# Attention, experts and gated MLP on one core: a pair's six value products as one team, and the second pair's keys and queries loaded ahead of w_in

## The chip, the core and the metric

The kernel runs on one core of a Trainium2 chip. The core has five engines that run side by side, each with its own queue of instructions: TensorE (PE, matmuls; PEld is its weight load), VectorE (DVE), ScalarE (ACT), GpSimd (POOL) and SyncE (SP, which here only issues transfers). They meet by semaphores. The metric is the device time of one launch in microseconds; before it is 493.17 us, the median of three runs (492.27 to 494.79).

## What is computed

```python
# attention: 4 batches, 12 heads, 448 positions, head width 64
scores = scale * np.matmul(q, k.transpose(0, 1, 3, 2))
scores = cap * np.tanh(scores / cap)
scores = scores - np.max(scores, axis=-1, keepdims=True)
attn = np.exp(scores)
attn = attn / (np.sum(attn, axis=-1, keepdims=True) + 1e-09)
return np.matmul(attn, v).astype(np.float32)
...
# 4 experts, each a causal attention of width 64 over x (768 wide); a token's best 2 are mixed
a = np.exp(scores)
a /= a.sum(-1, keepdims=True) + 1e-09
ye = a @ v @ wo[e]
...
# gated MLP: h = gelu(x @ w_in); u, v = halves of h; v normed, mixed over positions by w_sg
gated = u * v_s
return (x + gated @ w_out).astype(np.float32)
```

The attention's output is the experts' x, and theirs is the MLP's. w_in comes as 64-bit numbers, and the kernel multiplies it ahead of time with the experts' output weights.

## The kernel before

The attention goes through 24 pairs of heads (4 batches, 6 pairs each); two heads of width 64 share the 128 partitions. Positions are 448 = 3 x 128 + 64. For pair n the scores come in four blocks named s_n_0 to s_n_3: three of 128 keys each for both heads, and a fourth with the 64 keys left over, which serves two neighbouring pairs at once. Names in the program are s, batch, pair, block, number; the profile leaves batch and buffer number out and writes s. Each block is two banks of PSUM, and there are two such tiles (`ps_s`, bufs=2). `scores` (line 588) computes a block on TensorE, then ScalarE takes its tanh into p (tile p_n_0 holds blocks 0 and 1, p_n_1 blocks 2 and 3) and the exponential over the whole of p. VectorE adds up the blocks into pb, from which TensorE takes the row sums (`sums`, 650).

`values` (621) multiplies the exponentials with the values. For an even pair that is six products into po: three blocks of 128 keys (KB = 3) times two heads, which lie side by side in TensorE as tiles of 128 rows by 64 columns. For an odd pair there are first four products of the leftover keys of both pairs (operand vt, tiles of 64 by 64), and then six. A score block uses tiles of 64 by 128. In float32 each product is two passes, so a product of one block for both heads is four instructions in the profile (x4), and two in the order (x2).

`slot` (675) does one pair: it loads, computes the scores of pair i and the values of pair i - 1, and between them runs side work, which in the first ten slots is `prepare_weights` (1086): w_in in twelve parts u = 0 to 11, each loaded (wi_0w and so on), turned from 64 bits into a float32 (`convert`: tiles wi0m and wi0e, on VectorE, the first step of u > 1 on ScalarE) and multiplied with wt on TensorE (w2ps). Later slots have the projections (qk), the transposes (tr) and the expert attention (a, av) of the batch that is finished as side work.

All this is first recorded and not issued. `Agenda` (77) keeps for each operation its engine, an estimate of how long it takes and what it needs; `run` (398) lists the recorded operations by the order of a planner, `order`, which goes forward in time and picks for each engine what can begin first, by four sets of rules of which the one that ends first is kept. Each engine then has a fixed order of instructions. On TensorE the planner forms teams: products that follow one another, have the same tile shape and lie in cells of the array that don't overlap (line 265). `begin` (275) lets a team's first product start only when the operands of all its members are there. Before, the two products of a key block are one team, and the next block's, which use the same cells, another.

The hardware knows nothing of teams. Each engine takes its queue strictly in the order written, and an instruction waits at its head for its own semaphores only.

Loads go through SP's queue, with eight transfers in flight. The first pair is loaded by `load_pair` (536), which ends in

```python
            load_w(0)
...
        return qp, kp, load_v(b, hp)
```

so the order of the first transfers is keys of pair 0, first part of w_in, values of pair 0 (vv, vt), keys, queries and values of pair 1.

Of the kernel before, what the change touches and what calls it, by code (L numbers as in the profile page):

```python
# [41 lines left out]
def drain(gen):  # L42
    for _ in gen:
        pass
# [32 lines left out]
class Agenda:  # L77


    LATENCY = {"pe": 230.0, "act": 60.0, "dve": 60.0, "pool": 100.0, "sp": 60.0}  # L80
    SLACK, MARGIN = 1000.0, (150.0, 200.0)
    STATE = ("slots", "queue", "where", "left", "free", "grid", "fresh", "cfg", "bank", "lock", "pipe", "kept")
    RULES = ((100.0, 0.0, 100.0), (100.0, 0.0, None), (100.0, 20.0, 100.0), (60.0, 0.0, 100.0))
    OVERLAP = {"act": 100.0, "dve": 80.0, "pool": 27.0, "sp": 0.0}
# [15 lines left out]
    def state(self, new):  # L100
        held = {k: [list(x) for x in v] if k in ("grid", "fresh") else
                {q: list(x) if isinstance(x, list) else x for q, x in v.items()} if isinstance(v, dict) else v
                for k, v in ((k, getattr(self, k)) for k in self.STATE)}
        return held, {i: (list(self.ops[i]["took"]), *[self.ops[i].get(k) for k in ("at", "end")]) for i in new}
# [27 lines left out]
    def add(self, eng, f, args, kw):  # L132
        i, name = len(self.ops), f.__name__
# [7 lines left out]
        after, tiles = set(), []  # L141
# [15 lines left out]
        for these, those in self.behind.items():  # L157
            if any(x.startswith(these) for x in tiles):
                after.update(self.of[those])
        op = dict(i=i, eng=eng, call=lambda: f(*args, **kw), after=after, tiles=set(tiles), took=[], port=False,  # L160
                  rank=i + self.late)
        n = max(x.free_size() for x in ins[:2] + outs[:1])
        psum = any(x.space == PSUM for x in ins + outs)
# [8 lines left out]
        elif eng == "pe":  # L172
# [5 lines left out]
            r, c = half(st.partition_size()), half(outs[0].partition_size())  # L178
            if name == "transpose":
                r = c = 4  # L180
# [23 lines left out]
    def order(self, new, by_level, floor):  # L204
        ops, uses = self.ops, self.uses
# [4 lines left out]
        for i in reversed(new):  # L210
            op = ops[i]
            took = op["dur"] + self.LATENCY[op["eng"]]
            if "bytes" in op:
                took = 2100.0 + op["extra"] + op["pipe"]
            elif op["eng"] == "pe":
                took = op["dur"] + (0.0 if any(ops[j]["eng"] == "pe" for j in then[i]) else 220.0)
# [42 lines left out]
        gang, team = {}, []  # L259
        for i in new:  # L260
            op = ops[i]
            if op["eng"] != "pe":
                continue
            r, c, r0, c0 = op["cell"]
            if (r, c) == (4, 4) or not team or (r, c) != ops[team[0]]["cell"][:2] or any(
                    abs(r0 - ops[j]["cell"][2]) < r and abs(c0 - ops[j]["cell"][3]) < c for j in team):
                team = []
            team.append(i)
            gang[i] = team
# [46 lines left out]
        while todo:  # L316
            best = None
            for e, pool in pools.items():
# [13 lines left out]
                if e == "pe":  # L332
                    t, i = max(near, key=lambda x: (ops[x[1]]["bank"] == self.bank, ops[x[1]]["key"], -x[1]))
                elif e == "sp":
                    t, i = min(near, key=lambda x: x[1])
                else:
                    t, i = max(near, key=lambda x: (ops[x[1]]["key"], -x[1]))
# [3 lines left out]
            t, i = best  # L341
            op = ops[i]
# [11 lines left out]
            if e == "pe":  # L354
                r, c, r0, c0 = op["cell"]
# [64 lines left out]
def build(ctx: ExitStack, tc: tile.TileContext, a: dict):  # L420
# [35 lines left out]
    agenda = Agenda(tc)  # L456
# [4 lines left out]
    def dma(*args, **kw):  # L461
        return sp.dma_start(*args, **kw) if agenda.on else nc.sync.dma_start(*args, **kw)
# [24 lines left out]
    def scale(with_keys):  # L487
        dve.memset(tsc, 0.0)
        act.activation(tsc, tsc, AF.Tanh)
        dve.reciprocal(tsc, with_keys)  # L490
        dve.tensor_copy(capt, with_keys)
        dve.tensor_scalar(tsc, tsc, 1.0 / math.sqrt(D), None, op0=ALU.mult)
# [34 lines left out]
    def load_v(b, hp):  # L527

        vv = at.tile([128, 2, KB, D], F32, tag="vv", name=f"vv{b}_{hp}", bufs=3)
        dma(vv, a["v"][b, :, 2 * hp:2 * hp + 2])  # L530
        if hp % 2 == 0:
            vt[b, hp // 2] = at.tile([128, 2, D], F32, tag="vt", name=f"vt{b}_{hp}", bufs=2)
            dma(vt[b, hp // 2], a["vt"][b, hp // 2])
        return vv

    def load_pair(b, hp):

        qp = at.tile([128, S], F32, tag="qp", name=f"qp{b}_{hp}", bufs=3)
        kp = at.tile([128, S + 1], F32, tag="kp", name=f"kp{b}_{hp}", bufs=3)
        if (b, hp) == pairs[0]:  # L540
            for c in (slice(0, S // 2), slice(S // 2, S)):
                act.dma_start(qp[:, c], a["qT"][b, :, hp, c])
            for c in (slice(0, 128), slice(128, S + 1)):
                dma(kp[:, c], a["k_cap"][:, c])
            scale(kp[:, S:])
            load_w(0)
        else:
            dma(kp[:, :S], a["kT"][b, :, hp, :])
            dma(qp, a["qT"][b, :, hp, :])
        return qp, kp, load_v(b, hp)  # L550

    PARTED = 12

# [2 lines left out]
    def part(i):  # L556

        if PARTED <= i < len(pairs):
            parts[i] = []
            for x, t, h, l in zip(ld[i], "qk", 'va', 'vv'):  # L560
                xh, xl = (at.tile([128, S], F32R, tag=t + p, name=f"{t}{p}{i}", bufs=2) for p in "hl")
                rnd(h, xh, x[:, :S])
                rest(l, xl, x[:, :S], xh)
                parts[i].append((xh, xl))
# [56 lines left out]
    def values(b, hp, vv):  # L621


        i, w = hp // 2, hp % 2
        if w == 0:
            po = ps_o.tile([128, 512], F32, tag="po", name=f"po{b}_{hp}")
            for c in range(KB):
                for j in range(2):
                    mm(po[64 * j:64 * j + 64, :S], vv[:, j, c, :], pend[b, hp][c // 2][:, j, c % 2, :],
                       start=(c == 0), stop=False)  # L630
                yield 805.0
            po_t[b, i] = po
            return
        po = (po_t.pop((b, i)), ps_g.tile([128, 512], F32, tag="g", name=f"po{b}_{hp}"))
        v, p = vt.pop((b, i)), ptail.pop((b, i))
        for t in range(2):
            r = slice(64 * t, 64 * t + 64)
            for j in range(2):
                mm(po[t][64 * j:64 * j + 64, :S], v[r, j, :], p[r, j, :], start=(t == 1), stop=(t == 0))
        yield 805.0  # L640
        os_t[b, i] = ao.tile([128, 2, S], F32, tag="os", name=f"os{b}_{hp}", bufs=5)
        act.activation(os_t[b, i][:, 0, :], po[0][:, :S], AF.Copy)
        for c in range(KB):
            for j in range(2):
                mm(po[1][64 * j:64 * j + 64, :S], vv[:, j, c, :], pend[b, hp][c // 2][:, j, c % 2, :],
                   start=False, stop=(c == KB - 1))
            yield 805.0
        act.activation(os_t[b, i][:, 1, :], po[1][:, :S], AF.Copy)

    def sums(b, i):  # L650
        g = ps_g.tile([128, 512], F32, tag="g", name=f"sum{b}_{i}")
        for j in range(4):
            mm(g[32 * j:32 * j + 32, :S], ones, pend[b, 2 * i + j // 2][2][:, j % 2, :], start=True, stop=True)
        rs = sums_t[b, i] = ao.tile([128, S], F32, name=f"rs{b}_{i}", tag="rs", bufs=1)
        rnd("avv"[i], rs, g[:, :S])
        yield 870.0
# [15 lines left out]
    pairs = [(b, hp) for b in range(B) for hp in range(HP)]  # L672
    ld = {}

    def slot(i, side):

        if i == 0:
            ld[0] = load_pair(*pairs[0])  # L680
            ld[1] = load_pair(*pairs[1])
        if i + 2 < len(pairs):
            qk = [at.tile([128, n], F32, tag=t, name=f"{t}{i + 2}", bufs=3) for t, n in (("qp", S), ("kp", S + 1))]
            b, hp = pairs[i + 2]
            dma(qk[1][:, :S], a["kT"][b, :, hp, :])
            dma(qk[0], a["qT"][b, :, hp, :])
            ld[i + 2] = qk
        part(i + 1)
        if i < len(pairs):
            first = scores(*pairs[i], 0, *ld[i][:2])  # L690
            drain(islice(first, 2))
            side("a")
            drain(first)
        else:
            side("a")
        side("w")
        if i:
            b, hp = pairs[i - 1]
            drain(values(b, hp, ld.pop(i - 1)[2]))
        if 0 < i < len(pairs) - 1:  # L700
            b, hp = pairs[i + 1]
            ld[i + 1] = (*ld[i + 1], load_v(b, hp))
        side("a")
        if i < len(pairs):
            drain(scores(*pairs[i], 1, *ld[i][:2], None if i % 2 else ld[i + 1][:2]))
        if i == len(pairs):
            drain(sums(B - 1, HP // 2 - 1))
            spread(B - 1, HP // 2 - 1)
        side("p")
        if 0 < i < len(pairs):  # L710
            b, hp = pairs[i - 1]
            if hp % 2 == 1:
                drain(sums(b, hp // 2))
        if i < len(pairs):
            add_up(*pairs[i])
        side("n")
# [435 lines left out]
    with tc.tile_pool(name="pre", bufs=2) as pre:  # L1152
# [7 lines left out]
        load_w, beside_pre = prepare_weights(pre)  # L1160
# [282 lines left out]
```

## Time and profile before

| | |
|---|---|
| median of 3 runs | 493.17 us (492.27 to 494.79) |
| profiled execution | 492.94 us |
| its span | 491.1 us, 7664 instructions |
| TensorE busy | 484.3 us, 99% |
| VectorE busy | 362.2 us, 74% |
| ScalarE busy | 325.1 us, 66% |
| GpSimd busy | 47.8 us, 10% |

The profile is of one execution; its span is what the engines' records cover, and 1.8 us of the execution lie around it. A busy share is a mean over stages: the attention is over by about 250 us, and ScalarE's share falls from there on. Times in a row are from the span's start. Where one engine's next instruction starts before the end that a row gives for the last one, the two overlap in the engine, so the distance between starts is what an instruction takes of the engine's time.

### The profile page before, as it was taken

Reading aid. Unit: us, or ns where it says so; the run is one execution under the profiler, and the core shown is the slowest. Engines: PE = TensorE matmul, PEld = TensorE weight load, DVE = VectorE, ACT = ScalarE, POOL = GpSimd, SP = SyncE. Lnnn points to the kernel's source line nnn. Section 1 sums busy time; section 2 is a strip of 40 time slices with the busy share of each in tenths; the row PEclk is TensorE's granted clock in tenths of the full one; section 3 lists DMA queues with packets and bytes.
Section 4 is the critical chain, followed back from the end, with each engine's and each line's share of the span. In section 5 each row is a group of like instructions: output and inputs, shape, how many; then the busy total and the mean of one; then the engine's idle time right before and its main releaser. Section 6 shows DMA issues by size and latency. Waiting matters only on the chain.

```text
span 491.1 us, 7664 instructions
## 1 busy us (share of the span) xinstructions
PE 484.3 (99%) x2723; PEld 332.8 (68%) x2723; DVE 362.2 (74%) x796; ACT 325.1 (66%) x555; POOL 47.8 (10%) x61
## 2 busy tenths in 40 slices
PE   9999999999999999999999999999999999999996
PEld 3333333456556657675658797687898998999996
DVE  4999999777899898998756789729979929707000
ACT  6999968999869887788736766647555625513201
POOL 0000000000200303100201302033010200100000
PEclk9999999999999999999999999999999999999999
DMA  8986556555161624141046320161010110110122
GB/s 285 351 308 186 168 133 184 174 151 168 42 176 43 191 61 155 50 131 40 33 128 193 93 81 33 45 240 50 0 39 1 39 37 1 56 57 19 57 75 75
DMA packets 37301, 53.38 MB, mean 109 GB/s; under 512 B 7696, under 2 KB 32272, under 8 KB 37264
## 3 DMA queue, kind: packets, MB, share of 16 engines
q1 hardware_dynamic: 36832, 52.56, 33.9%
q8 instruction: 21, 0.34, 0.3%
q10 hardware_dynamic: 432, 0.34, 0.2%
q14 instruction: 16, 0.13, 0.1%
HBM read 41.97 MB, written 10.83 MB: 108 GB/s over the span
## 4 chain that ended last, share of the span: by engine, by line
PE 90%; DVE 4%; ACT 3%; DMA 1%; issue 1%; SPq 0%; ACTq 0%
PE o L449 18%; PE po L449 12%; PE qk L449 12%; PE s L449 11%; PE sp L449 7%; PE v L449 7%; PE a L449 4%; PE hv L449 4%; PE hu L449 4%; PE w2ps L449 4%; PE av L449 3%; PE tr L449 3%; ACT p L449 2%; PE sum L449 2%; DMA wi_0w<-in_w_in_dram 1%; DVE pb L449 1%
## 5 line engine op out<-in xcount | busy, mean ns | idle before, releaser
L449 ACT ACTIVATE p<-s,tsc 128x896 f32<-128x896 f32 (+1 forms) x85 | 82.3, 999 | 13.1 <-PE s L449 13.0
L449 ACT ACTIVATE p<-p,capt 128x1792 f32<-128x1792 f32 (+1 forms) x48 | 76.9, 1605 | 0.7
L449 PE MATMUL po<-p,vv 128*64 128x448 f32 x288 | 59.9, 548 | 0.1
L449 DVE TENSOR_TENSOR pb<-pb,p 128x896 f32<-128x896 f32 (+1 forms) x48 | 54.1, 1127 | 5.7 <-ACT p L449 5.1
L449 PE MATMUL s<-qp,kp 64*128 64x448 f32 (+2 forms) x244 | 46.4, 566 | 0.2
L449 PEld LDWEIGHTS po<-p,vv 128*64 128x64 f32 x288 | 18.3, 136 | 38.1 <-issue 30.1
L449 DVE CUSTOM_DVE_ANT_0 a<-a,neg 128x128 f32<-128x128 f32 (+3 forms) x56 | 24.7, 471 | 21.3 <-PE a L449 19.2
L449 ACT ACTIVATE ob<-o 128x448 f32<-128x448 f32 (+1 forms) x24 | 12.4, 534 | 37.9 <-PE o L449 34.9
L449 PE MATMUL qk<-xh,wqk_h 128*128 128x448 f32 x96 | 36.5, 380 | 0.1
L449 PEld LDWEIGHTS s<-qp,kp 64*128 64x128 f32 (+1 forms) x244 | 16.4, 171 | 28.0 <-issue 13.5
L449 PE MATMUL qk<-xh,wqk_l 128*128 128x448 f32 x96 | 34.9, 364 | 0.0
L449 ACT ACTIVATE pe<-a,m 128x128 f32<-128x128 f32 (+3 forms) x56 | 27.4, 496 | 9.7 <-DVE m L449 4.9
L449 DVE SCALAR_TENSOR_TENSOR vs<-sp,gln,bsg 128x448 f32<-128x448 f32 x16 | 10.7, 679 | 30.0 <-PE sp L449 29.9
L449 DVE TENSOR_TENSOR pb<-p 128x896 f32<-128x896 f32 x24 | 26.4, 1099 | 7.6 <-ACT p L449 4.8
L449 ACT ACTIVATE gsu<-gsu 128x448 f32<-128x448 f32 x16 | 9.3, 579 | 25.4 <-DVE gsu L449 25.4
L449 PE MATMUL a<-qk 64*128 64x128 f32 (+3 forms) x128 | 25.1, 452 | 0.9 <-ACT qk L449 0.6
L449 PEld LDWEIGHTS qk<-xh,wqk_h 128*128 128x128 f32 x96 | 18.0, 187 | 8.7 <-issue 3.7
L449 PE MATMUL sp<-sg_h,vh 128*128 128x448 f32 x64 | 23.6, 370 | 0.0
L449 PE MATMUL sp<-sg_l,vh 128*128 128x448 f32 x64 | 23.4, 365 | 0.0
L449 PE MATMUL qk<-xl,wqk_h 128*128 128x448 f32 x96 | 22.0, 364 | 0.0
L449 POOL TENSOR_TENSOR rstd<-rstd,mhalf 128x1 f32<-128x1 f32 (+1 forms) x16 | 11.4, 712 | 102.2 <-DVE rstd L449 102.0
L449 PE MATMUL v<-wvg_h,xh 128*128 128x260 f32 x72 | 21.1, 293 | 0.2 <-ACT pe L449 0.2
(272 smaller groups left out, 1200.7 us busy)
## 6 DMA issues: line engine op xcount, KB each, us to landing
rb<-rd SPq DMA_DIRECT2D x24, 224.0 KB, 4.2
kp<-in_kT_dram SPq DMA_DIRECT2D x23, 224.0 KB, 4.0
qp<-in_qT_dram SPq DMA_DIRECT2D x23, 224.0 KB, 4.2
out_dram<-ob SPq DMA_DIRECT2D x23, 224.0 KB, 1.9
vv<-in_v_dram SPq DMA_DIRECT2D x24, 192.0 KB, 3.5
wuw<-in_w_out_dram SPq DMA_DIRECT2D x5, 384.0 KB, 4.2
wud<-wuw SPq DMA_DIRECT2D x10, 192.0 KB, 3.6
ws<-in_wqk_dram SPq DMA_DIRECT2D x4, 384.0 KB, 5.5
```

The lines of the kernel that those rows point to most:

```text
L449: return tc.keep_in_program_order(f(*args, **kw))
```

## The change

Two things. Products recorded with the same value of `join` now form one team even where they use the same cells, so that the planner lets the first of a pair's six products start only when the operands of all six are there. And `load_pair` no longer loads values and w_in; `slot` loads, at its first call, keys and queries of both first pairs, then the first part of w_in, then the values of both.

```diff
+    join = None
...
-        op = dict(i=i, eng=eng, call=lambda: f(*args, **kw), after=after, tiles=set(tiles), took=[], port=False,
+        op = dict(i=i, join=self.join, eng=eng, call=lambda: f(*args, **kw), after=after, tiles=set(tiles), took=[], port=False,
                   rank=i + self.late)
...
-            if (r, c) == (4, 4) or not team or (r, c) != ops[team[0]]["cell"][:2] or any(
+            same = team and op["join"] is not None and op["join"] == ops[team[0]]["join"]
+            if not same and (r, c) == (4, 4) or not team or (r, c) != ops[team[0]]["cell"][:2] or not same and any(
                     abs(r0 - ops[j]["cell"][2]) < r and abs(c0 - ops[j]["cell"][3]) < c for j in team):
                 team = []
...
-            load_w(0)
...
-        return qp, kp, load_v(b, hp)
+        return qp, kp
...
+            agenda.join = f"po{b}_{hp}"
             for c in range(KB):
                 for j in range(2):
                     mm(po[64 * j:64 * j + 64, :S], vv[:, j, c, :], pend[b, hp][c // 2][:, j, c % 2, :],
                        start=(c == 0), stop=False)
                 yield 805.0
+            agenda.join = None
...
             ld[0] = load_pair(*pairs[0])
             ld[1] = load_pair(*pairs[1])
+            load_w(0)
+            ld[0] = (*ld[0], load_v(*pairs[0]))
+            ld[1] = (*ld[1], load_v(*pairs[1]))
```

The six products of an odd pair get the same two lines. The work is the same; the planner orders much of TensorE, ScalarE and VectorE anew up to about 250 us of the span, and from there TensorE's order is the same as before.

TensorE in the first 20 us, before: s0_1_0 is block 0 of pair 1 of batch 0, po0_0 the products of pair 0, p0_0_0 and p0_0_1 its exponentials.

```order
L449 MATMUL s0_0_3_131<-qp0_1_115,kp0_1_116 64x448 x2
L449 MATMUL po0_0_141<-p0_0_0_120,vv0_0_113 64x448 x4
L449 MATMUL s0_1_0_135<-qp0_1_115,kp0_1_116 128x448 x2
L449 MATMUL s0_1_1_136<-qp0_1_115,kp0_1_116 128x448 x2
L449 MATMUL po0_0_141<-p0_0_1_129,vv0_0_113 64x448 x2
L449 MATMUL po0_0_141<-p0_0_1_129,vt0_0_114 64x448 x2
L449 MATMUL po0_1_156<-p0_0_1_129,vt0_0_114 64x448 x2
L449 MATMUL s0_1_2_145<-qp0_1_115,kp0_1_116 128x448 x2
```

After:

```order
L451 MATMUL s0_0_3_131<-qp0_1_112,kp0_1_113 64x448 x2
L451 MATMUL s0_1_0_135<-qp0_1_112,kp0_1_113 128x448 x2
L451 MATMUL s0_1_1_136<-qp0_1_112,kp0_1_113 128x448 x2
L451 MATMUL po0_0_141<-p0_0_0_120,vv0_0_115 64x448 x4
L451 MATMUL po0_0_141<-p0_0_1_129,vv0_0_115 64x448 x2
L451 MATMUL po0_0_141<-p0_0_1_129,vt0_0_116 64x448 x2
L451 MATMUL po0_1_156<-p0_0_1_129,vt0_0_116 64x448 x2
L451 MATMUL s0_1_2_145<-qp0_1_112,kp0_1_113 128x448 x2
```

The first four products of pair 0 (eight instructions of the profile) stood ahead of s0_1_0 and s0_1_1, and now stand behind these, together with the other two.

VectorE's way to the second part of w_in, wi1m, before: wi0_1w is the part as loaded, pb0_0 the sums of pair 0's exponentials.

```order
L449 TENSOR_SCALAR wi1m_137<-wi0_1w_126 128x512
L449 TENSOR_SCALAR wi1m_137<-wi1m_137 128x512 x2
L449 SCALAR_TENSOR_TENSOR wi1m_137<-wi0_1w_126,wi1m_137 128x512
L449 TENSOR_SCALAR wi1e_138<-wi1m_137 128x512
L449 TENSOR_TENSOR pb0_0_125<-pb0_0_125,p0_0_1_129 128x896
L449 SCALAR_TENSOR_TENSOR wi1e_138<-wi0_1w_126,wi1e_138 128x512
L449 TENSOR_TENSOR pb0_0_125<-pb0_0_125,p0_0_1_129 64x896
L449 TENSOR_TENSOR wi1m_137<-wi1m_137,wi1e_138 128x512
L449 TENSOR_SCALAR wi2m_151<-wi2m_151 128x512
```

After:

```order
L451 TENSOR_SCALAR wi1m_137<-wi0_1w_126 128x512
L451 TENSOR_TENSOR wi0m_123<-wi0m_123,wi0e_124 128x512
L451 TENSOR_SCALAR wi1m_137<-wi1m_137 128x512 x2
L451 TENSOR_TENSOR pb0_0_125<-pb0_0_125,p0_0_1_129 128x896
L451 SCALAR_TENSOR_TENSOR wi1m_137<-wi0_1w_126,wi1m_137 128x512
L451 TENSOR_TENSOR pb0_0_125<-pb0_0_125,p0_0_1_129 64x896
L451 TENSOR_SCALAR wi1e_138<-wi1m_137 128x512
L451 TENSOR_SCALAR wi2m_151<-wi2m_151 128x512
L451 SCALAR_TENSOR_TENSOR wi1e_138<-wi0_1w_126,wi1e_138 128x512
L451 TENSOR_SCALAR wi2m_151<-wi2m_151 128x512
L451 TENSOR_TENSOR wi1m_137<-wi1m_137,wi1e_138 128x512
```

Two steps of the third part, wi2m, and the end of the first, wi0m, now stand between the steps of wi1m; its steps are also further apart.

TensorE in the third batch, around the projection qk0_1_1 of the expert work, before: s2_3_2 and s2_4_0 are score blocks, po2_2 products.

```order
L449 MATMUL po2_2_965<-p2_2_1_944,vv2_2_911 64x448 x2
L449 MATMUL s2_3_2_970<-qh15_932,kh15_934 128x448 x2
L449 MATMUL s2_3_2_970<-ql15_933,kh15_934 128x448 x2
L449 MATMUL s2_3_2_970<-qh15_932,kl15_935 128x448 x2
L449 MATMUL s2_4_0_984<-qh16_956,kh16_958 128x448 x2
L449 MATMUL s2_4_0_984<-ql16_957,kh16_958 128x448 x2
L449 MATMUL s2_4_0_984<-qh16_956,kl16_959 128x448 x2
L449 MATMUL qk0_1_1_971<-xh0_290,wqk_h_76 128x448
```

After, from the end of that projection (tr are transposes of the expert work):

```order
L451 MATMUL tr0_0_1_0_972<-ident_73,pe0_0_1_0_872 128x128
L451 MATMUL tr0_0_1_0_972<-ident_73,pe0_0_1_1_884 128x128 x2
L451 MATMUL tr0_0_1_2_973<-ident_73,pe0_0_1_2_907 128x128 x3
L451 MATMUL po2_2_965<-p2_2_0_936,vv2_2_911 64x448 x4
L451 MATMUL po2_2_965<-p2_2_1_944,vv2_2_911 64x448 x2
L451 MATMUL s2_3_2_970<-qh15_932,kh15_934 128x448 x2
L451 MATMUL s2_3_2_970<-ql15_933,kh15_934 128x448 x2
L451 MATMUL s2_3_2_970<-qh15_932,kl15_935 128x448 x2
L451 MATMUL s2_4_0_984<-qh16_956,kh16_958 128x448 x2
L451 MATMUL s2_4_0_984<-ql16_957,kh16_958 128x448 x2
L451 MATMUL s2_4_0_984<-qh16_956,kl16_959 128x448 x2
L451 MATMUL tr0_0_1_3_974<-ident_73,pe0_0_0_3_915 128x128 x4
```

Two score blocks stood ahead of the projection, with a third of pair 2's products; after, all three products of pair 2 and both blocks stand behind it and its transposes.

## Rows read from the trace of the kernel before

**Rows 1.** The page: busy time of the engines, and the chain that ended last

```profile
PE 484.3 (99%) x2723; PEld 332.8 (68%) x2723; DVE 362.2 (74%) x796; ACT 325.1 (66%) x555; POOL 47.8 (10%) x61
...
PE 90%; DVE 4%; ACT 3%; DMA 1%; issue 1%; SPq 0%; ACTq 0%
```

**Rows 2.** Busy time by stretch: start:end, length, busy us of each engine, PE clock, DMA

```profile
10.00:33.00 23.00, 22.77 (x115) 7.40 (x113) 22.73 (x39) 22.78 (x26) 0.00 (x0) 1.00 1.00 356
...
60.00:140.00 80.00, 80.00 (x460) 39.82 (x459) 67.36 (x120) 68.79 (x90) 3.79 (x4) 1.00 0.53 148
140.00:162.00 22.00, 21.80 (x150) 14.27 (x150) 20.55 (x39) 19.46 (x28) 2.62 (x3) 1.00 0.35 96
162.00:260.00 98.00, 97.15 (x661) 62.93 (x658) 80.42 (x192) 71.38 (x124) 12.51 (x12) 1.00 0.33 100
```

**Rows 3.** Timeline of SP: start us, us, queue line op out<-in xcount

```profile
7.22 0.33 SPq L449 DMA_DIRECT2D wi_1w<-in_w_in_dram  x1
...
8.13 0.43 SPq L449 DMA_DIRECT2D wt<-in_woT_dram  x1
...
9.15 0.37 SPq L449 DMA_DIRECT2D negf<-in_c_neg_dram  x1
```

**Rows 4.** Timeline of VectorE: start us, us, engine line op out<-in shapes xcount [idle before]

```profile
7.23 0.43 DVE L449 TENSOR_SCALAR wi0m<-wi_0w 128x512 int32<-128x512 int32 x1 [2.95 <-DMA wi_0w<-in_w_in_dram]
7.69 0.89 DVE L449 TENSOR_SCALAR wi0m<-wi0m 128x512 f32<-128x512 f32 x2
...
17.21 0.68 DVE L449 TENSOR_TENSOR wi1m<-wi1m,wi1e 128x512 f32<-128x512 f32 x1
17.82 0.41 DVE L449 TENSOR_SCALAR wi2m<-wi2m 128x512 f32<-128x512 f32 x1
```

**Rows 5.** Timeline of ScalarE at the start

```profile
8.17 1.79 ACT L449 ACTIVATE p<-p,capt 128x1792 f32<-128x1792 f32 x1
9.87 1.89 ACT L449 ACTIVATE p<-s,tsc 128x896 f32<-128x896 f32 x2
11.79 1.79 ACT L449 ACTIVATE p<-p,capt 128x1792 f32<-128x1792 f32 x1
```

**Rows 6.** Timeline of TensorE, 10 to 34 us

```profile
10.07 1.72 PE L449 MATMUL po<-p,vv 128*64 128x448 f32 x8
11.73 1.77 PE L449 MATMUL s<-qp,kp 64*128 64x448 f32 x8
13.63 0.97 PE L449 MATMUL po<-p,vv 128*64 128x448 f32 x4
14.54 0.98 PE L449 MATMUL po<-p,vt 64*64 64x448 f32 x8
15.45 1.77 PE L449 MATMUL s<-qp,kp 64*128 64x448 f32 x8
17.15 1.12 PE L449 MATMUL w2ps<-wi0m,wt 128*128 128x512 f32 x2
18.12 1.02 PE L449 MATMUL w2ps<-wi1m,wt 128*128 128x512 f32 x2
...
22.49 2.48 PE L449 MATMUL po<-p,vv 128*64 128x448 f32 x12
24.89 0.98 PE L449 MATMUL s<-qp,kp 64*64 64x448 f32 x8
...
31.87 2.14 PE L449 MATMUL s<-qp,kp 64*128 64x448 f32 x8
```

**Rows 7.** Timeline of ScalarE beside the projection of the third batch

```profile
149.52 1.89 ACT L449 ACTIVATE p<-s,tsc 128x896 f32<-128x896 f32 x2
151.30 1.04 ACT L449 ACTIVATE p<-p,capt 128x896 f32<-128x896 f32 x1
152.24 0.54 ACT L449 ACTIVATE qk<-qk 128x448 f32<-128x448 f32 x1
```

**Rows 8.** Timeline of TensorE behind that projection

```profile
152.82 0.66 PE L449 MATMUL tr<-ident,pe 128*128 128x128 f32 x4 [0.20 <-ACT qk L449]
```

More of the change, by code (lines that the diff above doesn't have):

```diff
@@ L642, in values @@
         act.activation(os_t[b, i][:, 0, :], po[0][:, :S], AF.Copy)
+        agenda.join = f"po{b}_{hp}"
         for c in range(KB):
@@ L647, in values @@
             yield 805.0
+        agenda.join = None
         act.activation(os_t[b, i][:, 1, :], po[1][:, :S], AF.Copy)
```

## The prediction

> **What bounds the kernel now.** I read the shares of the engines first. The reader is to see one number: TensorE is busy for 484.3 of 491.1 us, and the chain that ended last is TensorE for 90% [rows 1]. So the end moves by what the change puts into or takes out of TensorE's own row: rounds, changes of tile shape, and gaps. Second, the same by stage: from 10 to 33 us all three of TensorE, VectorE and ScalarE are within 0.3 us of full, and from 140 to 162 us VectorE and ScalarE have only 1.5 and 2.5 us of slack in 22; from 60 to 140 they have 11 to 13 us in 80 [rows 2]. An edit that makes VectorE or ScalarE late therefore shows at once in the first stretch and around 150 us, and is swallowed between. Nothing of TensorE's arithmetic is removed, so a gain can come only from gaps and tile shape changes, and before 260 us the gaps are few: TensorE's slack is 0.23 us in 10 to 33, none in 60 to 140, 0.2 in 140 to 162 and 0.85 in 162 to 260 [rows 2]. That limits the gain, before any detail is read, to these gaps and what the shape changes cost.
>
> **The load order.** SP has eight transfers in the air; each further issue starts when the transfer eight places earlier has landed. So SP's issue times tell landings: w_in's first part at 7.22, the head's last value tile before 8.13, second keys and second queries by 9.15 [rows 3]. VectorE confirms the first: it has been idle 2.95 us when it starts on w_in at 7.23 [rows 4]. Keys and queries took 9.15 - 8.13 = 1.02 us of the queue; now they go ahead, and w_in's first part lands about 1.0 us later, at 8.25. Bounds: 0 (if the transfers share the engines rather than follow one another) and 1.92 (9.15 itself). Everything behind vt_0 lands as before, since the same bytes are ahead of it. What the earlier keys buy: the second half of s_0_3 can be computed sooner, but ScalarE only reads it with the second of two tanh started at 9.87, and it runs through from 8.17 [rows 5]; so nothing.
>
> **The head of the products.** Before, TensorE uses the time in which it has no free score tile for the first eight product instructions (10.07), then does s_1_0 and s_1_1, then the other products when the second exponential ends at 11.79 + 1.79 = 13.58 [rows 5, 6]. As one team of a pair's products they can't go first any more: s_1_0 and s_1_1 come ahead, and these need the two score tiles. The first tanh of 9.87 ends at about 10.86, the second at 11.76 (the row holds two, 1.89). So s_1_0 starts at 10.91, s_1_1 at 11.81 and ends at 12.66 (1.70 for two blocks, 15.45 to 17.15). The twelve product instructions take 2.40 (22.49 to 24.89), to 15.06; the exponential of 13.58 is in time for the last four. The vt products take 0.91, to 15.97, where before had 15.45 [rows 6]: **+0.52**. That already has one tile shape change less in it: eight and four instructions apart took 1.66 + 0.91 = 2.57 against 2.40.
>
> **The first w_in products.** TensorE then does two score blocks (1.70) and the wi0m product (0.97) and wants wi1m at 18.64. VectorE before goes from 7.23 to 17.89 without a pause, 10.66 us, until wi1m is there [rows 4]. After, two wi2m steps stand ahead of it (0.41 long, some 0.35 apart, +0.7), while about five steps no longer directly follow the one that they read (0.46 from 7.23 to 7.69 for a step of 0.43, but 0.61 from 17.21 to 17.82 for one of 0.68: about 0.1 each, -0.5 to -0.6). So 10.75 or so from 8.25: 19.0, and TensorE starts at 19.1: **+0.5**. Bounds: 0 (w_in lands as before) and 1.3 (it lands at 9.15). Everything queued behind this product on TensorE, which takes its queue in order, waits with it.
>
> **The rest of the first two batches.** Joined products leave stretches in which score blocks follow one another with no products between. There are two score tiles, so a third block waits until ScalarE has emptied the first. Before shows one such case: at 31.87 two blocks take 2.14 where 1.77 is usual, +0.37 [rows 6]. In the new order I find three that look as tight (s_3_1 near 29 us; the second w_in part, where wi8m comes late, near 57; s_2_2 of the second batch near 79), and the old one is gone, since w_in products stand there now: 3 x 0.37 - 0.37 = **+0.74**. Lower bound 0 (each absorbed), upper 1.5 (twice as long each).
>
> **Around 150 us.** Before, both score blocks s_3_2 and s_4_0 of the third batch stand ahead of the projection qk, so ScalarE does their two tanh and an exponential (149.52 to 152.24) while TensorE projects [rows 7]; TensorE then waits only about 0.2 us, at 152.82 [rows 8]. After, the projection comes first, then the joined products, s_3_2, s_4_0. From the end of s_3_2 ScalarE has tanh, tanh, the half exponential, the copy of a transpose to pt and another tanh before s_4_3 can start: 0.89 + 0.89 + 0.94 + 0.54 (taken as the copy at 152.24) + 0.92 = 4.2, with some 0.2 for starting. TensorE has s_4_0, the transposes, s_4_1, a, s_4_2 and the vt products: three blocks of some 0.75 and 0.6, 0.15 and 0.9, 3.9 us. The last of these takes the PSUM tile that the pt copy frees, so it waits first; I take 1.0 us for both waits, less the 0.2 to 0.4 that go: **+0.7**. Bounds 0 and 1.75 (the two waits end to end).
>
> **Tile shapes.** From 13.63 to 14.54 four product instructions take 0.91, twelve take 2.40; so eight more take 1.49 and a change of shape costs 0.91 - 0.745 = 0.165 [rows 6]. I count 153 changes in the order of before, 149 after; one is in the head's term, the other three give **-0.5**. After about 250 us the order is the same on TensorE, so no term there.
>
> Sum: 0.52 + 0.5 + 0.74 + 0.7 - 0.5 = +1.96. The profiled execution took 492.94 (span 491.1 and 1.84 around it), so 494.9; the median of the three runs is 0.23 above that execution, so **495.1**.
>
> **Rivals.**
> Lateness that adds up (slower). VectorE starts w_in about 1.0 us later and from 10 to 60 us has next to no slack to catch up; each further w_in product would then find its operand late, not just wi1m. Place: the second w_in group near 57 to 60 us, which stands earlier in TensorE's order than before, with three score blocks and a pair's products no longer ahead of it. Price: wi1m at its bound 1.3, the three waits at 1.5 and 150 us at 1.3: 0.52 + 1.3 + 1.5 + 1.3 - 0.5 = +4.1, or half of the excess, +3.0: 496.2 to 497.3. It decides once the w_in group waits more than 0.8 us in all. For it: 22.73 busy of 23 on VectorE. Against: from 60 us on VectorE has 12.6 us of slack in 80 to catch up in, before the expert work begins [rows 2].
>
> No waits (faster side). The planner computed the new order with all the waits; where its durations are right, the score blocks come when tiles are free. Then the head costs 0.52, the rest nothing, and the waits that before has (0.37, 0.2) and three shape changes go: 0.52 - 0.57 - 0.5 = -0.55, 492.6. With the head's gap covered too and the waits of 162 to 260 us (0.85) gone, -1.9 and 491.3. More than 2.5 us would need more gaps than before has.
>
> The change doesn't do what it says: the hardware knows no team. The order only puts instructions next to each other, and the first product still starts on its own wait. Where all six were together anyway (22.49, twelve instructions) nothing differs. If only the head differs: 492.94 + 0.5 to 1.0 + 0.23 = 493.7 to 494.2.
>
> The clock. The granted clock is 1.00 in every stretch of before, 2.4 GHz, with no gap from 14 to 260 us above 1 us [rows 2]; the change puts new gaps of about 0.8 us at 10.1 and 0.5 at 18.6 into the stretch right behind the start. If the clock fell to its 1.2 GHz level from the first gap to the vt products, s_1_0, s_1_1 and the twelve products (1.70 + 2.40) would take twice as long: +4.1, or half where it returns midway: 497.2 to 499.2. Against: the gaps of before (1.0 us in the first 10 us, 0.2 behind) lie in stretches granted 1.00.
> The Trainium skill, TensorE: Matmul & The Clock Gate, section "A second HAM failure mode: psum-queue depth-cycling", speaks for this rival: brief idling between groups of matmuls that cycle through PSUM tiles made the clock swing in another kernel. No run here shows that.
>
> **How the numbers follow.** About 0.5%, 2.5 us, is what a measurement of this kernel tells from no change: faster is below 490.7, slower above 495.6. The forecast (terms as summed) has 0.52; its own range from the terms' bounds is 493.4 to 496.6, so a fifth of it lies above 495.6. Lateness 0.21, clock 0.04, no waits 0.13, only the head 0.10. Slower: 0.10 + 0.21 + 0.04 = 0.35. Faster: 0.06, out of "no waits", in case the terms I can't see from before go down. Same: 0.59. The range 491.8 to 497.8 leaves out the clock, the farther half of "no waits" and the worst of lateness.
>
> **What would show it.** Right: s_1_0 at about 10.9 and vt at 15.1 on TensorE; VectorE's first w_in step at 8.2 to 8.4; a wait of the w_in product near 19 on VectorE; a wait on ScalarE behind the projection near 155; and the stretch from 260 us on merely shifted. Wrong: w_in landing at 7.2 still; ScalarE idle where I have it as the releaser; a stretch in which the granted clock is below 1.00; or a shift that changes behind 260 us.

## The result and the profile after

The changed kernel takes 496.14 us (median of 7 runs, 495.30 to 497.16); before takes 493.62 us beside it (7 runs, 492.27 to 494.79). The ratio is 1.0052, 95% interval 1.0034 to 1.0070: slower, by 2.5 us. The line of 0.5% that the prediction draws lies inside this interval, so on which side of it the kernel is stays open. The profiled execution took 495.30 us with a span of 493.5, 2.4 more than before's.

The page of the changed kernel, beside [rows 1]: TensorE is busy for 0.6 us less and the span is longer, so against this profile all of the loss is waiting. Against a second profile of before (experiment 5: busy for 482.9 us, span 490.0) it is busy for 0.8 us more; 0.6 of that is a group of products near 157 us that takes 1.58 us instead of 0.98, since a part of it waits.

```profile
PE 483.7 (98%) x2723; PEld 331.6 (67%) x2723; DVE 360.9 (73%) x796; ACT 324.7 (66%) x555; POOL 47.5 (10%) x61
...
PE 89%; ACT 4%; DVE 4%; DMA 1%; issue 1%; SPq 0%; ACTq 0%
```

Busy time by stretch, columns as in [rows 2]:

```profile
10.00:33.00 23.00, 22.28 (x99) 7.64 (x100) 22.89 (x41) 22.05 (x24) 0.00 (x0) 1.00 1.01 351
...
60.00:140.00 80.00, 79.64 (x463) 39.82 (x463) 66.92 (x119) 68.65 (x88) 7.82 (x7) 1.00 0.49 141
140.00:162.00 22.00, 21.83 (x145) 12.84 (x146) 19.71 (x37) 19.01 (x28) 0.63 (x2) 1.00 0.42 115
162.00:260.00 98.00, 97.15 (x659) 61.90 (x658) 78.81 (x189) 72.64 (x124) 10.30 (x10) 1.00 0.29 86
```

TensorE's slack from 10 to 33 us went from 0.23 to 0.72 (the longest wait, 1.64 us, ends where this stretch begins), from 60 to 140 us from nothing to 0.36; the loss around 150 us doesn't show as slack here, since its wait lies inside a group of products in which half of the array goes on. What TensorE waited for, summed (us, times, longest):

```profile
PE s L451 <- ACT p L451: 3.0, 5, 1.6
...
PE w2ps L451 <- DVE wi1m L451: 0.4, 1, 0.4
```

The timeline of TensorE, for [rows 6]:

```profile
6.38 1.98 PE L451 MATMUL s<-qp,kp 64*128 64x448 f32 x12 [0.51 <-ACT p L451]
10.00 1.92 PE L451 MATMUL s<-qp,kp 64*128 64x448 f32 x8 [1.64 <-ACT p L451]
11.85 2.48 PE L451 MATMUL po<-p,vv 128*64 128x448 f32 x12
...
15.17 1.77 PE L451 MATMUL s<-qp,kp 64*128 64x448 f32 x8
...
18.41 1.13 PE L451 MATMUL w2ps<-wi1m,wt 128*128 128x512 f32 x2 [0.41 <-DVE wi1m L451]
...
21.18 1.77 PE L451 MATMUL s<-qp,kp 64*128 64x448 f32 x8
...
28.43 1.92 PE L451 MATMUL s<-qp,kp 64*128 64x448 f32 x8 [0.31 <-ACT p L451]
```

s_1_0 waits at 10.00 for the tanh of s_0_2. The 1.64 us are not all lost: before has eight product instructions there, which take 1.66 us [rows 6] and come later here. The twelve products follow in one piece at 11.85, wi1m is waited for at 18.41, and a third score block in a row waits at 28.43. The other engines at the start, ScalarE and VectorE (beside [rows 5] and [rows 4]):

```profile
7.26 1.79 ACT L451 ACTIVATE p<-p,capt 128x1792 f32<-128x1792 f32 x1
8.96 1.88 ACT L451 ACTIVATE p<-s,tsc 128x896 f32<-128x896 f32 x2
```

```profile
7.67 0.43 DVE L451 TENSOR_SCALAR wi0m<-wi_0w 128x512 int32<-128x512 int32 x1 [3.24 <-DMA wi_0w<-in_w_in_dram]
```

ScalarE is 0.91 us earlier than in [rows 5], VectorE 0.44 later on w_in than in [rows 4]. The first has nothing to do with the change: it comes from TensorE's first 7 us, which differ from run to run (experiment 5).

Around 150 us, TensorE and then ScalarE, for [rows 8] and [rows 7]:

```profile
154.33 0.66 PE L451 MATMUL tr<-ident,pe 128*128 128x128 f32 x4
155.15 0.47 PE L451 MATMUL s<-qh,kh 64*128 64x448 f32 x2 [0.17 <-ACT p L451]
...
156.86 1.58 PE L451 MATMUL po<-p,vt 64*64 64x448 f32 x8
158.37 1.08 PE L451 MATMUL s<-qp,kp 64*64 64x448 f32 x8
```

```profile
153.63 0.58 ACT L451 ACTIVATE kh<-kp 128x448 fp32r<-128x448 f32 x1 [1.57 <-PE s L451]
154.11 1.89 ACT L451 ACTIVATE p<-s,tsc 128x896 f32<-128x896 f32 x2
155.89 1.04 ACT L451 ACTIVATE p<-p,capt 128x896 f32<-128x896 f32 x1
156.83 0.59 ACT L451 ACTIVATE pt<-tr 128x512 f32<-128x512 f32 x1
157.30 1.01 ACT L451 ACTIVATE p<-s,tsc 128x896 f32<-128x896 f32 x1
```

ScalarE has nothing to do for 1.57 us until s_3_2 is there, and then its whole row of two tanh, an exponential, a copy and a tanh (154.11 to 158.2) is waited for: the vt products take 1.58 (two products wait inside the group for the copy at 156.83), s_4_3 comes at 158.37.

To place the loss I compare the two at points where TensorE has issued the same set of instructions in both orders and the next one is the same too; a number such as "287 in" counts the instructions issued before. "Again" is the second profile of the kernel before (experiment 5).

| point on TensorE | before | again | after | after - before | after - again |
|---|---|---|---|---|---|
| s_0_2, batch 0 | 7.20 | 6.23 | 6.38 | -0.81 | +0.15 |
| s_1_2 | 15.45 | 14.38 | 15.17 | -0.28 | +0.79 |
| s_2_1, behind the first w_in products | 20.79 | 19.82 | 21.18 | +0.39 | +1.36 |
| first score block of batch 1 | 53.09 | 51.98 | 53.64 | +0.55 | +1.66 |
| a score block of batch 1 (287 in) | 66.16 | 65.05 | 67.10 | +0.94 | +2.05 |
| s_2_3 of batch 1 | 78.37 | 77.25 | 79.64 | +1.27 | +2.39 |
| inside a score block of batch 1 (421 in) | 93.79 | 92.67 | 95.21 | +1.42 | +2.54 |
| a product (548 in) | 114.64 | 113.51 | 116.08 | +1.44 | +2.57 |
| last transposes before s_4_1, batch 2 | 152.82 | 151.70 | 154.33 | +1.50 | +2.63 |
| expert scores of batch 1 (937 in) | 172.02 | 170.90 | 174.67 | +2.65 | +3.77 |
| where the orders are the same again | 242.31 | 241.19 | 244.73 | +2.42 | +3.53 |

The steps from row to row agree within 0.15 us against either profile of before, but for the first row. From 242 us on the difference to the first profile stays at 2.4. From s_0_2 on the steps sum to 3.2 us (3.4 against the second profile), more than the 2.5 between the medians. The start isn't simply added to them: in experiment 7 s_0_2 comes 0.92 us later than in 8, s_2_1 only 0.14 (20.73 and 20.59), as 8 waits for wi1m and 7 does not. Both profiles of before (492.94, 491.80) also lie below the median of its runs, 493.62; where a usual run of it loses the rest, no profile here shows.

### The profile page after: what moved, and what is told of

Same layout as the page of the kernel before. It is cut to its first block, busy times and chain, and to the rows that moved or that the text cites. A ratio compares the mean times of both kernels' runs of the same rounds, so it can differ in the third digit from the quotient of the medians.

```text
span 493.5 us, 7641 instructions
## 1 busy us (share of the span) xinstructions
PE 483.7 (98%) x2723; PEld 331.6 (67%) x2723; DVE 360.9 (73%) x796; ACT 324.7 (66%) x555; POOL 47.5 (10%) x61
## 4 chain that ended last, share of the span: by engine, by line
PE 89%; ACT 4%; DVE 4%; DMA 1%; issue 1%; SPq 0%; ACTq 0%
PE o L451 18%; PE qk L451 12%; PE po L451 12%; PE s L451 10%; PE sp L451 7%; PE v L451 7%; PE a L451 4%; PE hv L451 4%; PE hu L451 4%; PE av L451 3%; ACT p L451 3%; PE w2ps L451 3%; PE tr L451 3%; PE sum L451 2%; DVE pb L451 1%; DMA wi_0w<-in_w_in_dram 1%
## 5 line engine op out<-in xcount | busy, mean ns | idle before, releaser
L451 DVE TENSOR_TENSOR pb<-pb,p 128x896 f32<-128x896 f32 (+1 forms) x48 | 52.4, 1092 | 11.5 <-ACT p L451 10.7
L451 PE MATMUL s<-qp,kp 64*128 64x448 f32 (+2 forms) x244 | 44.8, 558 | 2.8 <-ACT p L451 2.8
L451 PEld LDWEIGHTS s<-qp,kp 64*128 64x128 f32 (+1 forms) x244 | 15.2, 164 | 30.8 <-ACT p L451 17.4
L451 DVE SCALAR_TENSOR_TENSOR vs<-sp,gln,bsg 128x448 f32<-128x448 f32 x16 | 10.7, 679 | 30.0 <-PE sp L451 29.9
```

The lines of the kernel that those rows point to most:

```text
L451: return tc.keep_in_program_order(f(*args, **kw))
```

## The experiments

Each was timed in turns with the kernel before on the same chip; ratios are to before, edits to the changed kernel, but in 9 the edit is to the version of 7. The planner makes its order anew after each edit, so that other places can move too. A change to a line of `agenda.join` is made in both places, but for 3, where only even pairs are meant.

**1. The teams alone** (loads in the order of before).

```diff
             ld[0] = load_pair(*pairs[0])
             ld[1] = load_pair(*pairs[1])
-            load_w(0)
-            ld[0] = (*ld[0], load_v(*pairs[0]))
-            ld[1] = (*ld[1], load_v(*pairs[1]))
```

> The teams alone, with the loads in the order of before. Theory (the teams put score blocks ahead of the products, and TensorE then waits for ScalarE to empty the score tiles): most of the loss stays, 1.5 to 3 us over before (495 to 496.5), with s_1_0 still waiting near 10 us, no wait for wi1m near 18 us, and a loss of about 1.2 us between 152 and 160 us. Rival (the load order costs it, by making VectorE's w_in late): within 0.7 us of before.

496.64 us, ratio 1.0067 (1.0048 to 1.0087). So the loss is there with the teams alone; between 152 and 172 us its trace loses 1.1 us, as the changed kernel's does. Two rows of TensorE:

```profile
9.21 1.92 PE L451 MATMUL s<-qp,kp 64*64 64x448 f32 x8 [0.90 <-DMA qp<-in_qT_dram]
...
28.67 1.12 PE L451 MATMUL w2ps<-wi3m,wt 128*128 128x512 f32 x2 [1.41 <-DVE wi3m L451]
```

In the first, the second half of s_0_3 waits for the second queries, and TensorE has nothing else to do. Its first blocks went faster in this run (s_0_2 at 6.39), and the queries in their old place come after them. s_1_0 then starts at 10.11 with no wait of its own, where I had expected one. From s_0_2 to s_1_2 it takes 9.17 us, the changed kernel 8.79 (6.38 to 15.17), so the late queries cost 0.4 us here. The order differs from the changed kernel's between 19 and 80 us. The second is the wait for VectorE at the next w_in part, where I had put one of a score block.

**2. The load order alone** (the kernel before with the loads of the changed one; as against the changed kernel:)

```diff
-            agenda.join = f"po{b}_{hp}"
...
-        agenda.join = f"po{b}_{hp}"
```

> The load order alone, without teams. Theory: 0 to 0.7 us over before (at most what a wait for wi1m near 18 us costs, 0.5 to 0.7), with TensorE's order nearly that of before. Rival (the load order costs it): 1.5 to 2.5 us over before. The first half of it also tells whether w_in lands 0.5 to 1.0 us later by the load order alone.

492.97 us, ratio 0.9990 (0.9978 to 1.0003): no loss, so with 1 the loss is the teams'. The lateness is there all the same, on VectorE and then on TensorE:

```profile
8.43 0.43 DVE L449 TENSOR_SCALAR wi0m<-wi_0w 128x512 int32<-128x512 int32 x1 [3.54 <-DMA wi_0w<-in_w_in_dram]
```

```profile
9.28 1.72 PE L449 MATMUL po<-p,vv 128*64 128x448 f32 x8 [0.74 <-ACT p L449]
...
19.17 1.98 PE L449 MATMUL w2ps<-wi1m,wt 128*128 128x512 f32 x4 [0.77 <-DVE wi1m L449]
```

w_in starts at 8.43, wi1m is waited for 0.77 us; but the products begin at 9.28, 0.8 ahead of [rows 6]. At s_2_1 the two come to +0.30 against before, from 80 us on to -0.05; against the second profile of before (experiment 5) to +1.27 and +1.07. The traces alone would leave it open; the runs decide. Eleven of its twelve runs lie between 492.8 and 493.3, those of before between 492.1 and 495.2.

**3. The first pair no team.**

```diff
-            agenda.join = f"po{b}_{hp}"
+            agenda.join = None if (b, hp) == (0, 0) else f"po{b}_{hp}"
```

> The changed kernel, but the first pair's products are no team. Theory: the head's term (0.55) and a part of the wait for wi1m go, as the products of 10 us come back ahead of s_1_0: 0.6 to 1.2 us below the changed kernel, the loss of 152 to 160 us as there. Rival (the head is hidden behind ScalarE, which runs through, and the loss lies elsewhere): within 0.3 us of the changed kernel.

495.09 us, ratio 1.0037 (1.0023 to 1.0050): 0.15% or 0.7 us below the changed kernel's ratio, as the theory has it, though the intervals overlap. Its trace has the first eight products ahead of s_1_0 again (9.91), no wait for wi1m nor one near 28 us, and s_2_1 at 20.67, 0.5 ahead of the changed kernel in a run whose s_0_2 came 0.81 later.

**4. No teams in the third batch.**

```diff
-        agenda.join = f"po{b}_{hp}"
+        agenda.join = None if b == 2 else f"po{b}_{hp}"
```

> The changed kernel, but no teams in the third batch. Theory: its 1.15 us between 152 and 160 us go, with s_3_2 and s_4_0 ahead of the projection again: 0.5 to 1.2 us below the changed kernel, everything before about 115 us unchanged. Rival (this loss is time that TensorE loses anyway, since ScalarE is near full there): the loss shows up elsewhere in 115 to 170 us, within 0.3 us of the changed kernel.

495.62 us, ratio 1.0034 (1.0019 to 1.0050), 0.18% or 0.9 us lower. In the trace TensorE's order is the changed kernel's up to 116 us, where it runs 2.87 us behind (the reason follows); at the expert scores of batch 1 (937 in) it is 1.98 behind. So it gains 0.9 us, as the runs have it and as the theory says. In between it is 2.4 us behind at 137 us, 3.13 at the transposes before s_4_1 and 1.98 behind s_4_3: the loss between 152 and 172 us is gone, but TensorE loses 0.7 us just ahead of it that the changed kernel doesn't, and gains 0.5 ahead of that. The profile is worth more for what its start shows, w_in on VectorE and then TensorE:

```profile
9.38 0.43 DVE L451 TENSOR_SCALAR wi0m<-wi_0w 128x512 int32<-128x512 int32 x1 [5.00 <-DMA wi_0w<-in_w_in_dram]
```

```profile
20.12 1.20 PE L451 MATMUL w2ps<-wi1m,wt 128*128 128x512 f32 x2 [2.04 <-DVE wi1m L451]
21.11 1.91 PE L451 MATMUL w2ps<-wi0m,wt 128*128 128x512 f32 x2
22.82 1.84 PE L451 MATMUL w2ps<-wi1m,wt 128*128 128x512 f32 x2
24.59 1.77 PE L451 MATMUL s<-qp,kp 64*128 64x448 f32 x8
```

```profile
18.00:20.00 2.00, 0.07 (x1) 0.00 (x0) 2.00 (x6) 2.00 (x4) 0.00 (x0) 1.00 0.88 282
20.00:22.00 2.00, 1.88 (x4) 0.86 (x5) 2.00 (x5) 1.89 (x3) 0.00 (x0) 0.76 0.81 237
22.00:24.00 2.00, 2.00 (x4) 0.64 (x2) 2.00 (x5) 1.19 (x2) 0.00 (x0) 0.50 1.06 348
24.00:26.00 2.00, 2.00 (x9) 0.69 (x8) 1.94 (x3) 0.34 (x1) 0.00 (x0) 0.89 1.03 368
```

w_in landed at 9.38 instead of 7.67, with the same order of loads; the wait for wi1m became 2.04 us; and behind it the granted clock was 0.50 from 22 to 24 us, the 1.2 GHz level (the trace's record of it has this level from 21.0 to 24.5), after TensorE had done nothing from 18.1 to 20.1. From 20.12 to 24.59 it took 4.47 us for what takes 2.77 in the changed kernel (18.41 to 21.18): 1.7 us more. That is the rival of the clock, in one of the twelve executions profiled.

**5. The kernel before again.** No edit.

> The kernel before once more, unchanged, for a second profile of it. In the first one TensorE ran at half its rate until about 6.5 us, in the four later profiles of other kernels until about 4.1 to 5 us, with nothing in those kernels that differs ahead of 7 us. If that is chance from run to run, s_0_2 starts anywhere from 6.4 to 7.2 us here, and where it starts early the second half of s_0_3 has to wait for the second queries to land (near 9.1 us). If instead the order of the loads sets it, s_0_2 starts at 7.2 us again.

The profiled execution took 491.80 us (span 490.0; the first one 492.94 and 491.1), the runs 493.80 (8 runs, ratio 1.0000).

```profile
6.29 0.43 DVE L449 TENSOR_SCALAR wi0m<-wi_0w 128x512 int32<-128x512 int32 x1 [1.89 <-DMA wi_0w<-in_w_in_dram]
```

```profile
6.23 2.99 PE L449 MATMUL s<-qp,kp 64*128 64x448 f32 x12 [0.51 <-ACT p L449]
9.15 1.72 PE L449 MATMUL po<-p,vv 128*64 128x448 f32 x8
```

s_0_2 at 6.23 and not 7.20, in the same program: chance from run to run. The trace shows what differs. Its record of the granted clock begins, at 1.00, at 3.77 us here and at 6.61 in the first profile; a stretch without a record is printed as 1.00. In the first profile the first score instructions start 0.37 us apart, here 0.19; which level was granted ahead of the record isn't shown, but half the pace fits 1.2 GHz. In all twelve profiles the record begins between 3.75 and 6.61 us, and the six in which it does so by 4.2 us are the six with s_0_2 by 6.6.

The wait that I expected at s_0_3 was there, though shorter: the second half starts at 8.25, when the second queries have landed (SP's next issue, 8.22), and the row of 6.23 takes 2.99 us for the twelve instructions that take 1.98 in the changed kernel.

```profile
8.22 0.35 SPq L449 DMA_DIRECT2D negf<-in_c_neg_dram  x1
```

In the first profile it is the same, 9.17 and 9.15 [rows 3]. w_in, and with it all behind it, landed 0.94 us earlier than in [rows 4]. So a single profile of before is uncertain by 1 us from its first 7 us alone, and the 2.4 us between the two first profiles are 3.5 against this one; the medians, 2.5, lie between.

**6. Neither the first pair's team nor those of the third batch.**

```diff
-        agenda.join = f"po{b}_{hp}"
+        agenda.join = f"po{b}_{hp}" if b != 2 and (b, hp) != (0, 0) else None
```

> The changed kernel with neither the first pair's team nor those of the third batch. If the two terms stand for themselves, their gains add: 1.3 to 2.0 us below the changed kernel, a ratio of 1.001 to 1.003 to before, and what is left is the loss between 20 and 100 us. Rival (the gain of one was the gain of the other, TensorE losing to ScalarE in one place or another): no better than the better of the two, 1.0034 to 1.0037.

494.22 us, ratio 1.0014 (1.0002 to 1.0026): 0.38% or 1.9 us below the changed kernel. The gains of 3 and 4 (0.15% and 0.18%) add, within the intervals. Between 20 and 150 us one wait is left, in the second batch:

```profile
75.18 1.92 PE L451 MATMUL s<-qp,kp 64*128 64x448 f32 x8 [0.46 <-ACT p L451]
```

**7 and 8. Teams for seven pairs, and for one more.** The second line is 7, the third 8:

```diff
-        agenda.join = f"po{b}_{hp}"
+        agenda.join = f"po{b}_{hp}" if b == 3 or (b, hp) == (2, 0) else None
+        agenda.join = f"po{b}_{hp}" if b == 3 or (b, hp) in ((2, 0), (2, 2)) else None
```

> The load order, and teams only for the pairs of the last batch and for the first pair of the third. Theory (a team costs where it puts score blocks in a row on two tiles, and saves a change of tile shape where it doesn't): 0 to 1.2 us below before, 493.0 at most on the scale of 493.6 for before. Rival (teams cost wherever they are): 0.5 us or more above before.

> As the one before, with a team for one pair more, the third of the third batch, whose products then move with s_3_2 and s_4_0 behind the projection. Theory: this one team brings back the waits of 152 to 160 us: 1.0 to 2.0 us over the kernel without it, with TensorE's order the same up to about 138 us. Rival (the loss there comes from all of the batch's teams together): within 0.4 us of it.

7: 492.70 us, ratio 0.9979 (0.9968 to 0.9989), faster than before by 1.0 us. 8: 494.01 us, ratio 1.0008 (0.9994 to 1.0022), 1.3 us slower than 7. TensorE of 7, then of 8:

```profile
151.44 1.45 PE L451 MATMUL tr<-ident,pe 128*128 128x128 f32 x10
...
154.44 0.98 PE L451 MATMUL po<-p,vt 64*64 64x448 f32 x8
155.25 0.93 PE L451 MATMUL s<-qp,kp 64*64 64x448 f32 x8
```

```profile
152.74 0.47 PE L451 MATMUL s<-qh,kh 64*128 64x448 f32 x2 [0.18 <-ACT p L451]
...
154.44 1.58 PE L451 MATMUL po<-p,vt 64*64 64x448 f32 x8
155.95 1.08 PE L451 MATMUL s<-qp,kp 64*64 64x448 f32 x8
```

In 7 both score blocks and the products stand ahead of the projection, and ten transposes (151.44) run through where [rows 8] has a wait. In 8 the one team more brings the changed kernel's picture back: a wait at 152.74, vt products of 1.58, s_4_3 0.7 later. The two orders are the same up to 143 us. Between s_4_1 and s_4_3 8 loses 0.9 us to 7, and 0.7 more up to 242 us. Its order has 156 changes of tile shape against 150; five of the six lie behind 172 us, 0.8 us at the 0.165 worked out before. So this team costs by what the planner then moves, also far behind it, not by itself. The seven teams of 7 save little: TensorE's order is that of 2 up to 115 us, and from there to 242 us its trace gains 0.5 us on 2, 0.1%. The runs alone (0.9979 and 0.9990, intervals overlapping) don't tell the two apart.

**9. The same seven pairs, w_in ahead of the keys, the values behind them.**

```diff
             ld[0] = load_pair(*pairs[0])
-            ld[1] = load_pair(*pairs[1])
             load_w(0)
+            ld[1] = load_pair(*pairs[1])
```

> The version with teams for seven pairs, and another load order: first part of w_in, then keys and queries of the second pair, then the values of both. Theory (keys loaded ahead cost VectorE about 1 us at the start, which comes back as a wait for wi1m; the values are what can be late): w_in's first step at 6.3 to 7.3 us, no wait for wi1m, 0 to 0.7 us below the version with w_in behind the keys. Rival (where w_in stands is covered by other work): within 0.3 us of it, or above it by what the later keys cost.

492.65 us, ratio 0.9982 (0.9970 to 0.9994): the same as 7, the rival. w_in's first step was at 6.38 and there was no wait for wi1m, but 7 has none in its profile either.

**10. Without the first pair's team and those of the second and third batch.**

```diff
-        agenda.join = f"po{b}_{hp}"
+        agenda.join = f"po{b}_{hp}" if b == 3 or b == 0 and hp else None
```

> The changed kernel without the first pair's team and without those of the second and third batch. If the wait of score block s_2_2 of the second batch (near 76 to 79 us) is what is left of the loss with the first pair's and the third batch's teams out, it goes: 0.4 to 1.0 us below that version, a ratio of 0.999 to 1.0005 to before, with no wait of a score block on ScalarE between 60 and 100 us. Rival (the loss left over lies in the first batch): within 0.3 us of that version.

493.44 us, ratio 0.9996 (0.9984 to 1.0007), 0.18% or 0.9 us below 6, at the upper end of what I expected, and 0.56% below the changed kernel's. TensorE at the same place:

```profile
75.05 1.77 PE L451 MATMUL s<-qp,kp 64*128 64x448 f32 x8
76.76 1.98 PE L451 MATMUL w2ps<-wi11m,wt 128*128 128x512 f32 x4
```

No wait; the w_in products stand between the blocks again. Against 6 the trace gains 0.5 us at that wait, and another 0.5 between 76 and 150 us. Its start shows once more how w_in strays: first step at 9.15, a wait for wi1m of 1.15 us.

## Why the prediction was right, and where its sizes were off

The time came out at 496.14, 1.0 above the 495.1 forecast and inside the range; the loss of 2.5 us was forecast as 2.0. The line of 0.5%, beyond which I had given 0.35, lies inside the measured interval. That 2.0 and 2.5 are this close is in part luck: the places that the prediction adds up lose 3.2 to 3.4 us in the traces, and the medians differ by less. Step by step, with the steps of the table:

- **Bound by TensorE, only gaps count.** Right in the main: gaps make all of the loss against the first profile, 2.7 of 3.5 us against the second. The clock was misread: for the first 6.6 us of the profile of before the trace has no record of it (experiment 5), so that the gaps there say nothing against the clock's rival.
- **The load order.** w_in was to land 1.0 us later, at 8.25. Over the eight profiles with that order VectorE starts at 7.66 to 9.38, 8.2 in the mean; with w_in ahead (before, again, 1 and 9) at 6.29 to 7.28, 6.8 in the mean. The landing was right in the mean, but the shift is 1.4 us and not 1.0, as the profile that I read was among the late ones; and a single run strays by 1.7 us, once past my bound of 9.15. "What the earlier keys buy: nothing" failed for the kernel with teams: in experiment 1 TensorE waits 0.90 us for the queries in their old place, and 0.4 us of it is left at s_1_2. Without the first pair's team it holds within 0.1 us: from s_0_2 to s_1_2 it takes 8.25 and 8.15 us in the two profiles of before, 8.15 in 2 and 3. The load order as a whole costs nothing (2); whether it saves something beside the teams isn't shown (1 is 0.15% above the changed kernel, intervals overlapping, and its order differs).
- **The head, +0.52.** Measured 0.53 and 0.64 (from s_0_2 to s_1_2 against the two profiles). The order of waits was as worked out; the times lie 0.8 us earlier than the rows gave.
- **The first w_in products, +0.5.** Measured 0.57 to 0.67, a wait of 0.41 in the row and the restart behind it; 2.04 and 1.15 where w_in landed late (4, 10), 0.77 and 0.57 in 2 and 8, 0 in 3, 6 and 7. The way that the prediction sums up (10.75 us on VectorE) is confirmed: in all five profiles with this wait the product starts 10.7 to 10.8 us after VectorE's first step (7.67 and 18.41 in the changed kernel, 9.38 and 20.12 in 4).
- **The rest of the first two batches, +0.74.** This is the term that was mis-sized most: 1.05 between 21 and 115 us (1.21 against the second profile). The three places were the right ones: 28.43 waits 0.31, the second w_in part 0.13 for wi8m at 56.61, and s_2_2 of the second batch, where I had said 79 us:

```profile
78.69 1.98 PE L451 MATMUL s<-qp,kp 64*128 64x448 f32 x12 [0.36 <-ACT p L451]
```

  These waits sum to 0.80. What I left out is that a wait costs more than its own length in the row: the two blocks behind that of 28.43 take 1.92 where 1.77 is usual, and the row's end of an instruction lies behind the point where the next would have started. By the table the three cost 0.53 (+0.16 from 21 to 53 us, and the 0.37 of before that is gone [rows 6]), 0.39 (53 to 67) and 0.48 (67 to 95): 1.40 where I had 3 x 0.37 = 1.11. Less 0.37 that is 1.03.
- **Tile shapes, -0.5.** About half of it is seen. 153 and 149 changes were counted rightly, and behind the head's one more is saved by 115 us, one is added near 157 and three are saved behind 160 us. Those three should give 0.5 at 0.165; the difference falls from +2.68 at 161 us to +2.42 at 242, by 0.26.
- **Around 150 us, +0.7.** 1.15 in the table, by the mechanism given (the pt copy, then the tanh); experiments 4, 7 and 8 show that the teams of that batch, and one of them alone, bring it. It was taken too low: I let the wait inside the vt products overlap with the next, and the order has a tile shape change more there.
- **The same order from 250 us on.** Right: the shift is 2.42 at 242 us and 2.4 at the end.
- **Rivals.** "No waits" is refuted by the rows. "Lateness that adds up" didn't decide: the second w_in group waits 0.13 and not 0.8. "Only the head" is refuted by 4 and 10. The clock did fall, in experiment 4, at the second of the two gaps named (wi1m) and for 1.7 us; it didn't set the median, but a single run of these kernels can have it. The Trainium skill, TensorE: Matmul & The Clock Gate, section "A second HAM failure mode: psum-queue depth-cycling", tells of a kernel whose clock swings because TensorE idles briefly and often between groups of matmuls. The traces here don't show that: the waits of the changed kernel, up to 1.64 us, are followed by 1.00, and the one fall stands behind a single wait of 2.04 us.
- **The range.** "Its own range from the terms' bounds", 493.4 to 496.6, doesn't follow from the bounds as given: added up they are +0.02 and +4.57, 493.2 to 497.7.

## What to carry to other kernels

Where a planner orders a bound engine, a rule that seems to touch one kind of work (these products) is paid for where it moves other work: read from the order what now stands in a row on how many buffers, and sum the other engine's row from there to the first instruction that waits. Such a rule is best applied where its effect was looked at, not everywhere: with the new load order, seven of the 24 pairs as teams are 0.2% faster than before (by the traces about half of it the teams'), all 24 are 0.5% slower. And before a difference of 2 us between two profiles is explained, take a second profile of the kernel before.

## What the runs showed of the hardware

- The trace's record of the granted clock, at 1.00, began 3.75 to 6.61 us into the span, with the same instructions ahead in all twelve profiles. TensorE's first score instructions of 224 columns started 0.37 us apart in the first profile of before (6.61) and 0.19 apart in the changed kernel's (4.16); s_0_2 started at 7.20 and 6.38, over all twelve between 6.23 and 7.20.
- The first part of w_in reached VectorE between 7.66 and 9.38 us with one and the same order of loads, and between 6.29 and 7.28 with the other.
- After a wait of 2.04 us at 18.1 us the granted clock fell to 0.50 for 22 to 24 us (0.76 and 0.89 in the two stretches beside it); no other of the twelve profiles has a stretch below 1.00 before its last few microseconds.
